# Eight of sixteen weight loads issued from ScalarE's queue instead of SyncE's, in a fused linear attention and soft mixture-of-experts kernel

## The chip, the core and the metric

The kernel runs on one core of one Trainium2 chip. A core has a matrix engine (TensorE, PE in the profile; its weight loads are listed apart as PEld), three engines for element work (VectorE or DVE, ScalarE or ACT, GpSimd or POOL) and SyncE (SP), which in this kernel only issues transfers. Sixteen DMA engines move data between the chip's main memory (HBM) and the core's working memory (SBUF). Each engine runs its own instruction list in order, and the lists wait for one another by semaphores. The metric is the time of one execution on the device in microseconds (us); lower is better.

## What is computed

Linear attention without a softmax, a root-mean-square norm per head, and a soft mixture of experts over all 4608 tokens. The reference, shortened:

```python
def attn(q, k, v, g_norm):                       # 8 batches, 8 heads, 576 tokens, 64 wide
    kv = np.einsum('bhsd,bhse->bhde', k, v)
    out = np.einsum('bhsd,bhde->bhse', q, kv)
    rms = np.sqrt(np.mean(out * out, axis=-1, keepdims=True) + 1e-06)
    return out / rms * g_norm

def moe(x, phi, w1, w2):                         # x: 4608 x 512; 8 experts, 4 slots each, hidden 1024
    logits = x @ phi
    d = softmax over tokens of logits
    slot_input = (d.T @ x).reshape(8, 4, 512)
    for e in range(8):
        slot_out[e] = np.maximum(slot_input[e] @ w1[e], 0.0) @ w2[e]
    c = softmax over slots of logits
    return c @ slot_out
```

All inputs are 32-bit floats, and every one of them is read from HBM once.

## The kernel before

**Stages.** The 4608 tokens are cut into 36 tiles of 128 (`NT`), counted by `T`. First comes the loop over `T`: PE multiplies a tile of q with the block-diagonal kv matrices (`products`, L252 and, for the tile that straddles two batches, L243); ScalarE squares the result and copies it out of PE's accumulators (`square` L262, `evict` L269 and L270); VectorE, ScalarE and GpSimd make the norms, scale the tile and form its logits; groups of six tiles feed the softmax over tokens (`group_sum`, L386). In between, `kv_step` makes the kv matrix of the next batch (L184, L199). After the last tile the slot inputs are known, and the experts begin: `expert_h(e)` multiplies with w1 of expert e (L597) and ScalarE applies the ReLU (`h`, L605); `expert_y(e, hf)` multiplies with one half (`hf`) of w2's columns (L615) and adds into one accumulator per half. At last `output` multiplies each half with the softmax over slots (L647), ScalarE and VectorE copy the product to SBUF (L655, L657), and a transfer of 768 KB stores it (L658); there are six for each half, twelve in all.

**What is loaded, and in which order.** q and kv come as transfers of 1 to 2.25 MB (`load_q` L73, `load_kv` L69). The weights come as sixteen units of 2 MB: `("w1", e)` and `("w2", u)`, with e and u from 0 to 7. Each is one transfer of 128 rows of 16 KB, except `("w2", 2)`, which lies in two places and is two transfers of 128 rows of 8 KB. All are issued by `load_w` (L98) on SyncE, in the order w1 0, w2 0, w1 1, w2 1 (behind tile 18), w1 2, w1 3, w1 4 (behind tile 27), w1 5 (behind tile 31), w1 6, w1 7, w2 2 (after the loop), w2 3 (after `expert_h(0)`), w2 4, w2 5 (after `expert_h(1)` and both halves of expert 0), w2 6, w2 7 (after `expert_h(2)` and both halves of expert 1). The short names below are these. The units w2 2 to w2 7 are packed by column half: 2, 3 and 4 hold the first half for experts 2-3, 4-5 and 6-7, and 5, 6 and 7 hold the second half for the same experts.

**What sets the order.** The program is recorded in the order in which it is written, engine by engine; no scheduler moves anything. A load into SBUF space that was used before waits until that use is over (mostly a wait for PE). There are also eight completion semaphores, DMAHW0 to DMAHW7, dealt out in turn, so a transfer waits for the landing of the one that had its semaphore eight transfers earlier. SyncE carries out all of this in order: a load that waits holds up every later load and store.

**PE's order at the end**, on which the prediction leans: h of experts 0 and 1; y of expert 0, both halves; h 2; y of expert 1, both halves; h 3 to h 7; then y of experts 2 to 7 for the first half (needs w2 2, w2 3, w2 4); then y of expert 2, second half (w2 5), `mix(0)`, y of expert 3; outputs 0 and 1; y of experts 4 and 5, second half (w2 6); outputs 2 and 3; y of experts 6 and 7 (w2 7); output 4; `mix(1)`; outputs 5 to 11. In code:

```python
    for e in range(NE - LATE, NE):
        expert_y(e, 0)
    gather(0)
    expert_y(2, 1)
    mix(0)
    expert_y(3, 1)
    output(0, *chunks[0])
    output(0, *chunks[1])
    expert_y(4, 1)
    expert_y(5, 1)
```

Of the kernel before, what the change touches and what calls it, by code (L numbers as in the profile page):

```python
# [48 lines left out]
def soft_moe_linear_attention(ctx: ExitStack, tc: tile.TileContext, kv_in, q_in, w1_in, w2_in, c_in, out):  # L49


    nc = tc.nc
# [11 lines left out]
    def place(at, n):  # L64
        return arena[:, at * KB : at * KB + n]
# [22 lines left out]
    def homes(kind, u):  # L88
        at = W_AT[kind, u]
        if at is None:  # L90
            return [xflat[:, :UNIT]]
        return [place(a, UNIT // len(at)) for a in at]

    def load_w(kind, u):
        parts = homes(kind, u)
        n = UNIT // len(parts)
        for i, t in enumerate(parts):
            nc.sync.dma_start(t, (w1_in if kind == "w1" else w2_in)[u, :, i * n : i * n + n])  # L98

    def w_block(kind, u, i):  # L100
        parts = homes(kind, u)
# [20 lines left out]
    loads_behind = {  # L122
        9: lambda: (load_kv(5), load_kv(6), load_q(3), load_kv(7)),
        18: lambda: [load_w(k, e) for e in range(2) for k in ("w1", "w2")],
        27: lambda: [load_w("w1", e) for e in range(2, 5)],
        31: lambda: load_w("w1", 5),
    }

# [574 lines left out]
def build_program():  # L703
    import concourse.bacc as bacc

    nc = bacc.Bacc("TRN2", target_bir_lowering=False, num_devices=1, dynamic_dma_scratch_size=SCRATCH)
    shapes = {"kv": (B, P, TOK), "qt": (B // 2, P, TOK), "w1": (NE, P, UNIT), "w2": (NE, P, UNIT), "cs": (P, 129)}
    args = [nc.dram_tensor(f"in_{n}_dram", s, F32, kind="ExternalInput").ap() for n, s in shapes.items()]
    args.append(nc.dram_tensor("out_0_dram", (2, NCH, P, 2, 4 * CT * NS), F32, kind="ExternalOutput").ap())
    with tile.TileContext(nc, schedule_with_timeline_sim=True) as tc, tc.manual_schedule():  # L710
        soft_moe_linear_attention(tc, *args)
    return nc
# [43 lines left out]
```

## Time and profile before

| | us |
|---|---|
| median of 3 runs | 176.11 (175.97 to 177.55) |
| the profiled execution, own time | 175.97 |
| span of the profiled execution, first to last instruction | 174.2 |
| PE busy | 148.2 (85% of the span) |
| VectorE busy | 88.3 (51%) |
| ScalarE busy | 86.8 (50%) |
| GpSimd busy | 55.7 (32%) |
| moved by DMA | 71.68 MB, at a mean of 411 GB/s |

The busy times are shares of the span; a share says nothing by itself of what bounds a stage, since engines work beside each other. The page also has the span cut into 40 equal slices, with the busy tenths of each engine and of the DMA engines, and the chain of waits that ended last. A row of the timeline gives start, duration, engine, line, what is written and read, and in brackets how long the engine sat idle before it and what ended the wait. A row on a transfer gives how many were issued in the stretch asked for, their size, and the time from issue until the last byte was reported landed.

### The profile page before, as it was taken

How to read it: one execution, taken by the hardware profiler on the slowest of the kernel's cores; microseconds unless marked ns; L12 is line 12 of the kernel's file. 1: busy time of each engine (PE TensorE's matmuls, PEld its weight loads, DVE VectorE, ACT ScalarE, POOL GpSimd, SP SyncE). 2: the span in 40 equal slices, each digit the busy share in tenths (PEclk: the TensorE clock that was granted, in tenths of full speed). 3: DMA queues.
4: the chain of work that ended last, by engine and by line, in shares of the span. 5: the costliest groups of instructions: out<-in, count | busy, mean ns of one | idle time of the engine just before them, and what ended most of it. 6: DMA issues, size and time to landing. Idle time of an engine off the chain costs nothing.

```text
span 174.2 us, 4772 instructions
## 1 busy us (share of the span) xinstructions
PE 148.2 (85%) x2024; PEld 108.9 (63%) x2024; DVE 88.3 (51%) x180; ACT 86.8 (50%) x224; POOL 55.7 (32%) x65
## 2 busy tenths in 40 slices
PE   7577799999989899999999769989999959989500
PEld 5456778889779788888996555456556424445200
DVE  1122156566486565466663778733888114457600
ACT  2036286986957957878779553102234003336400
POOL 6000067656546676266773568000000000000000
PEclk9999999999999999999999999999999999999955
DMA  5999999999999999999999999999999999999994
GB/s 188 416 429 426 439 414 432 420 432 440 414 432 423 421 431 420 420 427 436 429 418 419 433 418 433 429 429 406 440 421 419 425 425 426 386 398 406 419 419 199
DMA packets 6645, 71.68 MB, mean 411 GB/s; under 512 B 736, under 2 KB 864, under 8 KB 2400
## 3 DMA queue, kind: packets, MB, share of 16 engines
q1 hardware_dynamic: 6624, 71.37, 97.5%
q8 instruction: 16, 0.26, 0.6%
q14 instruction: 5, 0.04, 0.1%
HBM read 61.93 MB, written 9.44 MB: 410 GB/s over the span
## 4 chain that ended last, share of the span: by engine, by line
PE 46%; DMA 20%; ACT 11%; DVE 11%; issue 3%; POOL 2%; SPq 1%; POOLq 0%; DVEq 0%
PE o L252 17%; DMA arena<-in_w_dram 11%; DMA arena<-in_kv_dram 9%; PE kvp_kv L184 8%; PE po L647 5%; PE pY L615 4%; PE ph L597 3%; DVE logits L329 3%; PE pS L386 2%; DVE ms L275 2%; ACT arena L655 2%; POOL part L324 2%; ACT bd L219 2%; PE o L243 2%; ACT sq L262 2%
## 5 line engine op out<-in xcount | busy, mean ns | idle before, releaser
L252 PE MATMUL o<-bd,arena 128*128 128x192 f32 x256 | 49.4, 336 | 1.4 <-ACT xall L270 0.6
L252 PEld LDWEIGHTS o<-bd,arena 128*128 128x128 f32 x256 | 40.8, 190 | 4.7 <-ACT xall L270 1.6
L302 POOL TENSOR_TENSOR xall<-xall,r 128x512 f32<-128x512 f32 x34 | 34.8, 1044 | 0.0
L324 POOL TENSOR_TENSOR part<-part,r 128x512 f32<-128x512 f32 x17 | 17.8, 1049 | 51.5 <-DVE r L293 51.5
L329 DVE TENSOR_REDUCE logits<-part 128x64 f32<-128x512 f32 (+1 forms) x19 | 19.3, 1015 | 16.1 <-POOL part L324 16.0
L275 DVE TENSOR_REDUCE ms<-sq 128x16 f32<-128x1024 f32 (+1 forms) x19 | 22.0, 1156 | 6.2 <-ACT sq L262 6.2
L262 ACT ACTIVATE sq<-o 128x512 f32<-128x512 f32 x36 | 21.5, 596 | 6.5 <-PE o L252 5.9
L270 ACT COPY xall<-o 128x512 f32<-128x512 f32 x34 | 20.6, 607 | 0.0
L184 PE MATMUL kvp_kv<-arena 128*64 128x64 f32 x480 | 17.3, 225 | 3.6 <-DMA arena<-in_kv_dram 3.6
L655 ACT COPY arena<-po 128x768 f32<-128x768 f32 x12 | 9.3, 800 | 20.2 <-DMA arena<-in_w_dram 10.3
L184 PEld LDWEIGHTS kvp_kv<-arena 128*64 128x64 f32 x480 | 15.2, 138 | 6.5 <-DMA arena<-in_kv_dram 4.5
L615 PE MATMUL pY<-arena,xall 128*32 128x256 f32 x256 | 15.2, 380 | 2.4 <-DMA arena<-in_w_dram 2.4
L657 DVE COPY arena<-po 128x768 f32<-128x768 f32 x12 | 11.3, 956 | 8.0 <-PE po L647 7.2
L647 PE MATMUL po<-logits,z 32*128 32x384 f32 x96 | 13.7, 526 | 1.6 <-ACT arena L655 1.0
L615 PEld LDWEIGHTS pY<-arena,xall 128*32 128x32 f32 x256 | 8.0, 110 | 9.1 <-issue 3.2
L597 PE MATMUL ph<-arena,sTe 128*32 128x256 f32 x224 | 12.7, 379 | 0.3 <-DVE sTe L544 0.3
L269 ACT COPY part<-o 128x256 f32<-128x256 f32 x34 | 12.6, 371 | 0.0
L386 PE MATMUL pS<-xall,d 128*32 128x129 f32 x288 | 10.7, 276 | 2.1 <-ACT d L374 2.1
L283 ACT ACTIVATE r<-ms,eps 128x16 f32<-128x16 f32 x17 | 5.2, 308 | 12.8 <-DVE ms L275 12.6
L647 PEld LDWEIGHTS po<-logits,z 32*128 32x128 f32 x96 | 6.3, 183 | 8.2 <-ACT arena L655 4.1
L291 DVE SCALAR_TENSOR_TENSOR r<-ms,r 128x16 f32<-128x16 f32 x17 | 3.0, 175 | 15.3 <-ACT r L284 15.3
L597 PEld LDWEIGHTS ph<-arena,sTe 128*32 128x32 f32 x224 | 7.2, 110 | 5.2 <-DVE sTe L544 0.6
(88 smaller groups left out, 143.9 us busy)
## 6 DMA issues: line engine op xcount, KB each, us to landing
arena<-in_w_dram SPq DMA_DIRECT2D x14, 2048.0 KB, 20.7
arena<-in_kv_dram SPq DMA_DIRECT2D x6, 2304.0 KB, 30.4
out_dram<-arena SPq DMA_DIRECT2D x12, 768.0 KB, 6.5
arena<-in_kv_dram SPq DMA_DIRECT2D x4, 1152.0 KB, 10.1
arena<-in_qt_dram SPq DMA_DIRECT2D x2, 2304.0 KB, 32.1
arena<-in_qt_dram SPq DMA_DIRECT2D x2, 1280.0 KB, 23.2
arena<-in_qt_dram SPq DMA_DIRECT2D x2, 1024.0 KB, 16.4
xall<-in_w_dram SPq DMA_DIRECT2D x1, 2048.0 KB, 15.4
```

The lines of the kernel that those rows point to most:

```text
L184: nc.tensor.matmul(self.pkv[lo : lo + 64, w, g], lhsT=main[:, w, 1, c, lo : lo + 64], rhs=main[:, w, 0, c, lo : lo + 64], start=c == 0 and ...
L252: nc.tensor.matmul(o[:, r, :192], lhsT=q_main(2 * g + i)[:, r, at : at + P], rhs=bds[i][:, r], start=True, stop=True)
L262: nc.scalar.activation(sqs[s][:, T - starts[s]], o[:, :, 32:160], AF.Square, scale=0.125)
L270: nc.scalar.copy(xts[T % NX][:, :, :128], o[:, :, 32:160])
L275: nc.vector.tensor_reduce(out=mss[s], in_=sqs.pop(s).rearrange("p t j (w d) -> p (t j w) d", w=2), axis=AX.X, op=ALU.add)
L302: nc.gpsimd.tensor_tensor(out=x, in0=x, in1=r[:, i].rearrange("p (j w) -> p j w", w=2).unsqueeze(3).to_broadcast([P, 4, 2, D]), op=ALU.mult,)
L324: engine.tensor_tensor(out=part, in0=part, in1=rs_of[s].unsqueeze(3).to_broadcast([P, STAGES[s], H, NS]), op=ALU.mult)
L329: nc.vector.tensor_reduce(out=L[:, pos(starts[s]) : pos(starts[s]) + STAGES[s]], in_=parts.pop(s).rearrange("p t h n -> p t n h"), axis=AX ...
L386: nc.tensor.matmul(pS[32 * j : 32 * j + 32], lhsT=ds[G][:, i], rhs=x[:, j], start=i == 0, stop=i == GROUPS[G] - 1)
L597: nc.tensor.matmul(ph[32 * j : 32 * j + 32], lhsT=sTe[:, (4 * e + c) * NS : (4 * e + c + 1) * NS], rhs=w_block("w1", e, 4 * c + j), start= ...
L615: nc.tensor.matmul(pY[32 * j : 32 * j + 32, hf, :256], lhsT=hTs[e][:, c], rhs=w_block("w2", u, at + c), start=e == 0 and c < 4, stop=e == ...
L647: nc.tensor.matmul(po[:, u, : CT * NS].rearrange("p (g x) -> p g x", g=2), lhsT=z[lo : lo + 32, f * P : (f + 1) * P], rhs=cT[k][lo : lo + 32],
```

## The change

`load_w` looks up each weight unit in a set, `ACT_LOADS`. The eight units in the set are issued from ScalarE's instruction list (`nc.scalar`), the other eight from SyncE's as before. The two lists have a queue each on the same sixteen DMA engines. Sizes, places, and the calls of `load_w` stay the same.

```diff
+    ACT_LOADS = {("w2", 0), ("w2", 1), ("w1", 3), ("w1", 5), ("w1", 7), ("w2", 3), ("w2", 5), ("w2", 7)}
+
     def load_w(kind, u):
+        queue = nc.scalar if (kind, u) in ACT_LOADS else nc.sync
         parts = homes(kind, u)
         n = UNIT // len(parts)
         for i, t in enumerate(parts):
-            nc.sync.dma_start(t, (w1_in if kind == "w1" else w2_in)[u, :, i * n : i * n + n])
+            queue.dma_start(t, (w1_in if kind == "w1" else w2_in)[u, :, i * n : i * n + n])
```

Three lines are added, so line numbers behind them grow by three (L98 becomes L101). On SyncE, from the last loads of q and kv to the stores, the list changes as follows ("-" before, "+" now; `in_w_dram` are the weights, `arena` and `xall` places in SBUF, x9 means nine in a row):

```order
 L73 DMA arena<-in_qt_dram 128x4608
 L69 DMA arena<-in_kv_dram 128x4608
-L98 DMA arena<-in_w_dram 128x4096 x9
-L98 DMA xall<-in_w_dram 128x4096
-L98 DMA arena<-in_w_dram 128x2048 x2
-L98 DMA arena<-in_w_dram 128x4096 x5
-L658 DMA out_dram<-arena 128x1536 x12
+L101 DMA arena<-in_w_dram 128x4096 x5
+L101 DMA arena<-in_w_dram 128x2048 x2
+L101 DMA arena<-in_w_dram 128x4096 x2
+L661 DMA out_dram<-arena 128x1536 x12
```

SyncE now issues w1 0, w1 1, w1 2, w1 4, w1 6, the two parts of w2 2, w2 4 and w2 6, and then the twelve stores.

On ScalarE, at the first experts, the list before reads (h is the ReLU of an expert, ph its product on PE, `logits` the exponential for the softmax over slots):

```order
L605 ACTIVATE h_1482<-ph_1465,rs 128x256 [waits DVE_49,PE_49,Pool_49]
L605 ACTIVATE h_1503<-ph_1486,rs 128x256 [waits PE_49]
L569 ACTIVATE logits<-logits 128x416 [waits DVE_49]
L605 ACTIVATE h_1552<-ph_1535,rs 128x256 [waits PE_49,Activation_49]
L569 ACTIVATE logits<-logits 128x416 [waits DVE_49]
```

and now:

```order
L608 ACTIVATE h_1482<-ph_1465,rs 128x256 [waits DVE_49,PE_49,Pool_49]
L101 DMA arena<-in_w_dram 128x4096 [waits DMAHW5_49,DMAHW1_49]
L608 ACTIVATE h_1503<-ph_1486,rs 128x256 [waits PE_49]
L101 DMA arena<-in_w_dram 128x4096 [waits DMAHW6_49,DMAHW2_49]
L572 ACTIVATE logits<-logits 128x416 [waits DVE_49]
L608 ACTIVATE h_1552<-ph_1535,rs 128x256 [waits PE_49,Activation_49]
L101 DMA arena<-in_w_dram 128x4096 [waits DMAHW0_49]
L572 ACTIVATE logits<-logits 128x416 [waits DVE_49]
```

The three transfers that came in are w2 3, w2 5 and w2 7, behind the ReLU of experts 0, 1 and 2. In front of each stands a wait for landings: DMAHW5 is that of w1 2, DMAHW6 that of w1 4, DMAHW0 that of w1 5, and DMAHW1 and DMAHW2 are those of w1 0 and w1 1, whose space is written over. The other five stand earlier on ScalarE: w2 0 and w2 1 behind the copies of tile 18, w1 3 behind those of tile 27, w1 5 behind those of tile 31, and w1 7 behind the last square root of the norms, where it waits for PE's last reading of its space. PE, VectorE and GpSimd keep their lists; the waits there name other DMAHW semaphores, since these are dealt out anew.

## The prediction

> **What bounds the kernel now.** I read the page's slices first, then the stretches of the second half, then the chain that ended last, then PE's rows at that place. The slices (40 of 4.36 us) show the DMA engines full from the second slice to the last but one:
>
> ```profile
> span 174.2 us, 4772 instructions
> ...
> DMA  5999999999999999999999999999999999999994
> GB/s 188 416 429 426 439 414 432 420 432 440 414 432 423 421 431 420 420 427 436 429 418 419 433 418 433 429 429 406 440 421 419 425 425 426 386 398 406 419 419 199
> ```
>
> The stretches have, per row, the busy time of five engines, the granted clock, the DMA engines' share, and GB/s:
>
> ```profile
> core 0: us, PE busy (x) PEld busy (x) DVE busy (x) ACT busy (x) POOL busy (x), PEclk, DMA share, GB/s
> ...
> 125.00:146.00 21.00, 18.31 (x310) 10.18 (x300) 10.42 (x24) 4.18 (x9) 0.00 (x0) 1.00 1.00 424
> 146.00:151.00 5.00, 4.75 (x52) 2.15 (x52) 2.00 (x3) 1.98 (x3) 0.00 (x0) 1.00 0.97 402
> 151.00:157.00 6.00, 5.49 (x60) 2.67 (x58) 3.52 (x5) 1.97 (x4) 0.00 (x0) 1.00 0.95 393
> 157.00:172.00 15.00, 6.08 (x44) 2.91 (x42) 5.67 (x7) 4.42 (x6) 0.00 (x0) 0.76 0.99 406
> ```
>
> From 125 to 146 the share is 1.00, and the slices say the same of what lies before: the transfers bound the kernel, and PE waits for them. Afterwards it drops to 0.95 to 0.99: here the stores come out of PE, ScalarE and VectorE only about as fast as they can be written. The chain shows that join (start, duration, what):
>
> ```profile
> 125.29 19.77 DMA arena<-in_w_dram
> ...
> 145.07 0.81 ACT arena L655
> ...
> 146.84 1.86 PE pY L615 x32
> ```
>
> So the end is set twice, by bytes and by the chain of outputs that starts at the late halves of w2. PE's rows name the wait before that chain:
>
> ```profile
> 133.68 5.36 PE L615 MATMUL pY<-arena,xall 128*32 128x256 f32 x96
> 141.48 1.07 PE L615 MATMUL pY<-arena,xall 128*32 128x256 f32 x16 [2.44 <-DMA arena<-in_w_dram]
> ...
> 146.77 1.93 PE L615 MATMUL pY<-arena,xall 128*32 128x256 f32 x32
> ```
>
> 133.68 is y of experts 2 to 7, first half, 5.36/3 = 1.8 us per pair, so the pair that needs w2 4 begins at 137.2. 141.48 is y of expert 2, second half, released by w2 5. 146.77 are experts 4 and 5, which need w2 6.
>
> **When the weights land now.** Issue rows of w1 6, w2 4 and w2 6 (in this order), each followed by the row with its size and the us to landing:
>
> ```profile
> 102.10 0.33 SPq L98 DMA_DIRECT2D arena<-in_w_dram  x1
> arena<-in_w_dram SPq DMA_DIRECT2D x1, 2048.0 KB, 14.7
> ...
> 121.84 0.33 SPq L98 DMA_DIRECT2D arena<-in_w_dram  x1
> arena<-in_w_dram SPq DMA_DIRECT2D x1, 2048.0 KB, 14.6
> ...
> 125.29 0.33 SPq L98 DMA_DIRECT2D arena<-in_w_dram  x1
> arena<-in_w_dram SPq DMA_DIRECT2D x1, 2048.0 KB, 20.9
> ```
>
> w1 6 lands at 116.8, w2 4 at 136.4, w2 6 at 146.2. Between the first and the last lie six units in 29.4 us: 4.9 us a unit, strictly one behind the other. w2 7 is due one unit after w2 6, at 151.1.
>
> **Cost on ScalarE.** Each issue takes 0.33 us on SyncE (rows above) to 0.42 (the row of kv 7 below); ScalarE gets eight, some 3 us. Behind each place it sits idle today (the bracket is the idle time before the row):
>
> ```profile
> 63.27 0.60 ACT L262 ACTIVATE sq<-o 128x512 f32<-128x512 f32 x1 [1.11 <-PE o L252]
> 86.61 0.31 ACT L283 ACTIVATE r<-ms,eps 128x16 f32<-128x16 f32 x1 [1.05 <-DVE ms L275]
> 98.11 0.31 ACT L283 ACTIVATE r<-ms,eps 128x16 f32<-128x16 f32 x1 [2.04 <-DVE ms L275]
> 111.79 0.32 ACT L362 ACTIVATE diag<-ident,rmax 128x32 f32<-128x32 f32 x1 [3.41 <-DVE rmax L358]
> 118.44 0.47 ACT L605 ACTIVATE h<-ph,rs 128x256 f32<-128x256 f32 x1 [4.90 <-PE ph L597]
> 120.12 0.47 ACT L605 ACTIVATE h<-ph,rs 128x256 f32<-128x256 f32 x1 [1.20 <-PE ph L597]
> 122.20 0.55 ACT L569 ACTIVATE logits<-logits 128x416 f32<-128x416 f32 x1 [1.61 <-DVE logits L568]
> 126.58 0.55 ACT L569 ACTIVATE logits<-logits 128x416 f32<-128x416 f32 x1 [2.48 <-DVE logits L568]
> ```
>
> In order: w2 0 and w2 1 (0.84 us) before the first row, w1 3, w1 5, w1 7, then (rows six to eight) w2 3, w2 5, w2 7. Every gap is longer than its issue: cost 0. With the cover gone it would be 3 us at most on the path of PE, which today waits 2.44 us for w2 5 anyway. SyncE's eight fewer issues are worth 0 too, since it waits most of the time; w2 2, w2 4 and w2 6 no longer queue behind w1 7, w2 3 and w2 5, and the stores no longer behind w2 7.
>
> **New waits.** Each of the three late issues holds up ScalarE's next ReLU or `logits` until older weights have landed. Taking turns, bytes move at the same rate, so w1 4, the eighth unit that either queue begins behind kv 7 (with part of a ninth beside it), is in at 71.3 (below) + 9 x 4.9 = 115.4 at the latest, and ScalarE asks at 120.12 + 0.47 = 120.6. These waits cost 0.
>
> **What the second queue delays.** w2 0 and w2 1, issued from ScalarE near 62.2 (63.27 - 1.11), no longer stand behind kv 7, which is needed at the row of L184 below:
>
> ```profile
> 36.00 0.42 SPq L69 DMA_DIRECT2D arena<-in_kv_dram  x1
> arena<-in_kv_dram SPq DMA_DIRECT2D x1, 2304.0 KB, 35.3
> ...
> 84.10 0.39 PE L184 MATMUL kvp_kv<-arena 128*64 128x64 f32 x6
> ```
>
> It lands at 71.3 now. Sharing half and half from 63.6 stretches the rest from 7.7 to 15.4 us, to 79.0: still 5 us ahead. Cost 0.
>
> The end is another matter. The total of bytes is unchanged and neither queue runs dry, so the last weight still lands at 151.1; but of two transfers that share, each lands later than if it had gone first. w1 7 goes out from ScalarE after 108.4 (gap of the fourth row above: 111.79 - 3.41) and is through by 120. w2 3 is issued at 118.9 and, with 1.4 us to its start (half of the 2.75 us that the first load, last fence below, takes beyond its moving), begins at 120.3. From there 30.8 us of moving remain: 14.7 for ScalarE's w2 3, w2 5, w2 7, and 16.1 for SyncE's rest of w1 6 (1.4), w2 2, w2 4, w2 6.
>
> - Equal bytes: SyncE's queue runs at half rate, w1 6 to 123.1, w2 2 to 132.9, w2 4 to 142.7; ScalarE's three end at 149.7, and w2 6 at 151.1.
> - Equal turns, row by row: w2 2 has rows of 8 KB against 16 KB, so its 4.9 us take 14.7, to 137.8. By then ScalarE's queue has moved 11.2 of 14.7; the other 3.5 are shared until 144.8, and w2 4, with 1.4 left, lands at 146.2, w2 6 at 151.1.
>
> PE's pair on w2 4 then ends 1.8 us after it, and y of expert 2 starts at 144.5 or 148.0, late by 3.0 or 6.5. In the first case w2 6 (151.1 against 146.77 + 3.0) makes it 4.3; in the second it is there in time. So the chain of outputs is late by 4.3 to 6.5 us, and what is late next is the stores. Once the weights are in, only this chain feeds the DMA engines.
>
> The Trainium skill ("DMA: Bandwidth & Descriptors", section "Queues, rings and completion order") says that each DMA engine goes round robin between queues packet by packet, a packet being typically 9 to 17 descriptors. By that a turn could be a whole unit's share of an engine (8 rows and a completion), which gives w2 4 at 146.2 as well, the later of the two. No run shown here has two data queues at work.
>
> How much of the delay reaches the end follows from the sixth and the last store, and from the first load, which had nothing ahead of it:
>
> ```profile
> 157.17 0.33 SPq L658 DMA_DIRECT2D out_dram<-arena  x1
> out_dram<-arena SPq DMA_DIRECT2D x1, 768.0 KB, 5.1
> ...
> 164.74 0.64 SPq L658 DMA_DIRECT2D out_dram<-arena  x1
> out_dram<-arena SPq DMA_DIRECT2D x1, 768.0 KB, 8.5
> ...
> 0.74 0.37 SPq L69 DMA_DIRECT2D arena<-in_kv_dram  x1
> arena<-in_kv_dram SPq DMA_DIRECT2D x1, 1152.0 KB, 5.5
> ```
>
> The sixth lands at 162.3, the last at 173.2: six in 10.9 us, 1.8 each, so from the sixth on the writing sets the pace. The sixth itself took 5.1 us; into an idle queue it would take 1.8 plus something between 0 and the first load's 5.5 - 2.75 = 2.75 us. The slack before a late chain shows at the end is thus 0.5 to 3.3 us; with no row nearer to either end I take the middle, 1.9. Sum: 4.3 - 1.9 = +2.4 us, or 6.5 - 1.9 = +4.6; the middle is +3.5. The execution profiled took 175.97 us, 0.14 below the median: 175.97 + 3.5 = 179.5. Its own range is +1.0 (equal bytes, all slack) to +6.0 (row turns, least slack): 177.0 to 182.0.
>
> **Rivals.**
> - The second queue changes nothing: the units come through one after another, w2 4 by 139.7 (141.48 - 1.8) and w2 6 by 148.7 (146.77 and the slack), and bytes bind as before. Time 176.0, within 0.5. For it: a share of 1.00 before 146, which no queue can improve or harm while it is fed. Against: w2 4 would have to pass two units issued before it. The Trainium skill's section "Issuing engines are not separate DMA queues" of the same page speaks for this and against any gain: all issuing engines use the same sixteen DMA engines, and a second one saves only issue time. The share of 1.00 agrees.
> - Turns cost time. The one foreign traffic in the trace is instruction fetches:
>
> ```profile
> q1 hardware_dynamic: 6624, 71.37, 97.5%
> q8 instruction: 16, 0.26, 0.6%
> ```
>
>   0.6% of 16 engines' 174.2 us over 16 packets of 16 KB is 1.05 us each, against 4.9/8 = 0.61 for a weight row: 0.44 more. Of a unit's 128 rows each engine moves 8, so ScalarE's eight units are 64 rows on each; if every one paid that, 28 us: 204. An eighth of it on top of the forecast is 183. Against: instructions go elsewhere than data.
> - ScalarE is held up. If w1 4 came after 120.6, the ReLU of expert 2 and all behind it would be late with it. It decides only from 9 us on (137.2 to 146.2, where PE waits anyway): each further us adds one, 180 and more.
> - Faster: two queues move more. The best slice has 440 GB/s, the stretch up to 146 424. Over the 87.5 us from 63.6 to 151.1 that would take 3.0 us off: 173. It decides (over 1%) from 434 GB/s, and only if w2 4 and w2 6 come no later than now. Against it, the share leaves no idle time to win.
>
> **How the numbers follow.** About 1% is what a measurement here can tell from no change. Forecast 0.52, of which 0.07 lies below that bound; nothing changes 0.25; turns cost 0.13; ScalarE held up 0.04; faster 0.06. Slower by over 1%: 0.45 + 0.13 + 0.04 = 0.62; within 1%: 0.32; faster: 0.06. The range 175.4 to 183.5 holds the forecast and nearly all of the second case, and leaves out the faster case and most of the dear turns.
>
> **What would show it.** Right: in the changed profile PE waits before the pair on w2 4 (L618), y of expert 2 starts at 144 to 148, DMA share below 0.95 between 147 and 157, w2 0 lands before kv 7, and no DMA wait on ScalarE's rows before the outputs. Wrong: y of expert 2 near 141.5 (rival one), GB/s under 400 between 64 and 146 (turns cost), L608 waiting for a DMA (ScalarE held up), GB/s over 434 (faster).

## The result and the profile after

The changed kernel takes 182.55 us (median of 4 runs, 180.88 to 184.51), the kernel before 176.04 (175.91 to 177.55): a ratio of 1.032, 95% interval 1.021 to 1.042, so slower. The forecast was 179.5 with a range of 175.4 to 183.5. Here and below, a ratio compares the means of those executions that lie within 1.5% of the fastest of their kernel (here without 184.51), so it need not be the ratio of the medians. The profiled execution after took 183.07 us with a span of 181.0; of before it was 175.97 and 174.2.

The page's slices of the kernel after (40 of 4.53 us) show where the time lies:

```profile
span 181.0 us, 4774 instructions
...
PEclk9999999999999999999999999999999579999975
DMA  6999999999999999999999999999999970889993
GB/s 200 414 428 422 443 416 438 411 442 407 444 428 423 421 422 427 425 429 416 438 424 418 431 424 434 420 411 425 434 422 424 431 319 36 348 349 403 414 414 162
```

Up to the 32nd slice nothing differs from before: engines full, 407 to 444 GB/s. Then there is a hole (36 GB/s) that was not there, and just ahead of it the granted clock of TensorE dips to a half. The stretches, with the columns of before (busy time of the five engines, granted clock, DMA share, GB/s):

```profile
64.00:100.00 36.00, 35.16 (x502) 29.63 (x494) 22.00 (x46) 27.26 (x77) 19.62 (x21) 1.00 1.00 425
...
125.00:146.00 21.00, 14.22 (x254) 9.66 (x250) 9.00 (x21) 3.36 (x7) 0.00 (x0) 0.87 1.01 428
146.00:151.00 5.00, 4.46 (x58) 1.88 (x50) 0.85 (x2) 0.00 (x0) 0.00 (x0) 0.87 0.51 216
151.00:157.00 6.00, 5.75 (x64) 2.63 (x60) 2.36 (x3) 2.01 (x3) 0.00 (x0) 1.00 0.54 221
```

Between 146 and 157 the share is 0.51 and 0.54, where it was 0.97 and 0.95. Only the engines that are behind still load (w2 6 lands at 151.2, w2 7 at 151.3), and there is nothing to store until 153.06, because PE is late. PE's rows at that place say what it waited for:

```profile
134.20 3.66 PE L618 MATMUL pY<-arena,xall 128*32 128x256 f32 x62
144.65 3.19 PE L618 MATMUL pY<-arena,xall 128*32 128x256 f32 x32 [6.78 <-DMA arena<-in_w_dram]
148.38 1.07 PE L618 MATMUL pY<-arena,xall 128*32 128x256 f32 x16 [0.54 <-DVE y L634]
149.38 0.70 PE L638 MATMUL pz<-y,sel 128*128 128x256 f32 x2
```

The first row is two pairs; the second is the pair on w2 4, which was due straight behind them and now waits 6.78 us. Behind it y of expert 2, second half, starts at 148.38, against 141.48. The chain that ended last agrees (start, duration, what; these rows are the longer pieces of that stretch):

```profile
122.37 22.14 DMA arena<-in_w_dram
144.65 3.23 PE pY L618 x32
148.38 1.07 PE pY L618 x16
153.74 1.86 PE pY L618 x32
```

The issues of the late units, each with the row of its time to landing, for w2 3 and w2 5 (ScalarE) and w2 4 (SyncE, whose issue row groups w2 4 and w2 6):

```profile
118.83 0.34 ACTq L101 DMA_DIRECT2D arena<-in_w_dram  x1
arena<-in_w_dram ACTq DMA_DIRECT2D x1, 2048.0 KB, 13.0
...
120.48 0.33 ACTq L101 DMA_DIRECT2D arena<-in_w_dram  x1
arena<-in_w_dram ACTq DMA_DIRECT2D x1, 2048.0 KB, 21.6
...
122.37 3.78 SPq L101 DMA_DIRECT2D arena<-in_w_dram  x2
arena<-in_w_dram SPq DMA_DIRECT2D x1, 2048.0 KB, 22.1
```

w2 3 lands at 131.8 and w2 5 at 142.1, within 0.8 us of before, but w2 4 at 144.5 instead of 136.4: it now lands behind w2 5, which PE needs only in the step after it. How the two queues shared can be read from their packets, bytes and share of engine time between 123 and 129, where SyncE's queue (q1) moves the rest of w2 2 in rows of 8 KB, and ScalarE's (q10) moves w2 3 in rows of 16 KB:

```profile
q10 hardware_dynamic: 105, 1.72, 67.8%
q1 hardware_dynamic: 96, 0.84, 33.5%
```

About as many packets each, but twice the bytes for the queue with the longer rows. The 96 are 59 rows of 8 KB, 15 packets of 4 bytes that report an engine's share of a transfer as done, and 22 rows of 16 KB, since the engines that are ahead have already begun w2 4. The packets of the trace show the turns themselves: sorted by start and end they form sixteen chains without gaps, one for each engine, and between 124 and 142 us 522 of 540 neighbours in a chain come from different queues. One row of one queue is followed by one row of the other.

### The profile page after: what moved, and what is told of

Same layout as the page of the kernel before. It is cut to its first block, busy times and chain, and to the rows that moved or that the text cites. A ratio compares the mean times of both kernels' runs of the same rounds, so it can differ in the third digit from the quotient of the medians.

```text
span 181.0 us, 4774 instructions
## 1 busy us (share of the span) xinstructions
PE 149.7 (83%) x2024; PEld 111.2 (61%) x2024; DVE 88.2 (49%) x180; ACT 86.9 (48%) x224; POOL 55.6 (31%) x65
## 4 chain that ended last, share of the span: by engine, by line
PE 50%; DMA 21%; ACT 11%; DVE 8%; issue 3%; POOL 2%; SPq 1%; POOLq 0%; DVEq 0%
PE o L255 16%; DMA arena<-in_w_dram 12%; DMA arena<-in_kv_dram 8%; PE kvp_kv L187 8%; PE pY L618 6%; PE po L650 6%; PE pS L389 3%; PE fill L432 3%; PE ph L600 2%; ACT arena L658 2%; DVE logits L332 2%; POOL part L327 2%; ACT bd L222 2%; PE o L246 2%; ACT sq L265 2%
## 5 line engine op out<-in xcount | busy, mean ns | idle before, releaser
L618 PE MATMUL pY<-arena,xall 128*32 128x256 f32 x256 | 17.4, 405 | 7.3 <-DMA arena<-in_w_dram 6.8
L618 PEld LDWEIGHTS pY<-arena,xall 128*32 128x32 f32 x256 | 9.3, 116 | 14.5 <-issue 9.9
L600 PEld LDWEIGHTS ph<-arena,sTe 128*32 128x32 f32 x224 | 8.4, 110 | 4.1 <-DVE sTe L547 0.6
```

The lines of the kernel that those rows point to most:

```text
L600: nc.tensor.matmul(ph[32 * j : 32 * j + 32], lhsT=sTe[:, (4 * e + c) * NS : (4 * e + c + 1) * NS], rhs=w_block("w1", e, 4 * c + j), start= ...
L618: nc.tensor.matmul(pY[32 * j : 32 * j + 32, hf, :256], lhsT=hTs[e][:, c], rhs=w_block("w2", u, at + c), start=e == 0 and c < 4, stop=e == ...
```

## The experiments

Times are medians, each with the ratio to the kernel before in the same session. That kernel's own median was 177.35, 176.03 and 176.02 us in the three sessions; the last two experiments bear on why it moves.

**The early five alone.** w2 3, w2 5 and w2 7 go back to SyncE.

```diff
-    ACT_LOADS = {("w2", 0), ("w2", 1), ("w1", 3), ("w1", 5), ("w1", 7), ("w2", 3), ("w2", 5), ("w2", 7)}
+    ACT_LOADS = {("w2", 0), ("w2", 1), ("w1", 3), ("w1", 5), ("w1", 7)}
```

> Five units stay on ScalarE's queue (w2 0, w2 1, w1 3, w1 5, w1 7), the last three (w2 3, w2 5, w2 7) go back to SyncE. Theory: the loss comes only from w2 2 and w2 4 sharing with units that are needed later; here the last units come one behind the other again, so w2 4 lands by 137, y of expert 2 (second half) starts near 141.5, and the span is 174 to 175. Rival (each unit on the second queue costs by itself): five eighths of the 6.8 us of span remain, 178.4.

Measured: 176.37 us, ratio 0.999 (0.995 to 1.002). The five early transfers on the second queue cost nothing and win nothing. Its profiled execution took 216.64 us at a granted clock of 0.65 and can't be compared row by row; the same kernel, profiled once more:

> The same kernel as that with five units on ScalarE's queue, for a profile at full clock: w2 2 to w2 7 land about 4.9 us apart, w2 4 by 137, w2 6 by 147, y of expert 2 (second half) near 141.5, span 174 to 175. Rival: 178.4.

Its span is 175.7 us and its time 177.81. w2 4, w2 5 and w2 6 land at 136.4, 141.3 and 146.2, as before. Its PE rows show that 1.5 us were lost at another place:

```profile
141.45 1.20 PE L618 MATMUL pY<-arena,xall 128*32 128x256 f32 x16 [2.38 <-DMA arena<-in_w_dram]
142.58 1.22 PE L638 MATMUL pz<-y,sel 128*128 128x256 f32 x2
143.73 1.94 PE L618 MATMUL pY<-arena,xall 128*32 128x256 f32 x16
```

The weights come as in the kernel before, but the matmuls behind the wait are slower: 1.94 us for 16 against 1.07. This is taken up in the last two experiments.

**The late three alone.** The reverse set.

```diff
-    ACT_LOADS = {("w2", 0), ("w2", 1), ("w1", 3), ("w1", 5), ("w1", 7), ("w2", 3), ("w2", 5), ("w2", 7)}
+    ACT_LOADS = {("w2", 3), ("w2", 5), ("w2", 7)}
```

> Only the last three units (w2 3, w2 5, w2 7) go out from ScalarE. Theory: the turns at the end are as in the changed kernel, w2 2 near 134, w2 4 between 144 and 146, y of expert 2 (second half) near 148, span 180 to 182. Rival (each unit costs by itself): three eighths of 6.8 us, 176.8.

Measured: 183.01 us, ratio 1.033 (1.026 to 1.039): the whole loss, with a span of 181.1 as expected. The wait on w2 4 is there again:

```profile
144.36 3.43 PE L618 MATMUL pY<-arena,xall 128*32 128x256 f32 x32 [6.91 <-DMA arena<-in_w_dram]
148.34 1.07 PE L618 MATMUL pY<-arena,xall 128*32 128x256 f32 x16 [0.54 <-DVE y L634]
```

**Short rows on ScalarE's queue.** If the queues take turns row by row, ScalarE's late units in rows of 8 KB should leave SyncE's queue half of the bytes, and w2 4 should come earlier. If they share bytes, nothing should move. Each of the three is split into two homes, and so into two transfers.

```diff
-    ("w2", 3): (72,), ("w2", 5): (104,), ("w2", 7): (136,),
+    ("w2", 3): (72, 80), ("w2", 5): (104, 112), ("w2", 7): (136, 144),
```

> The changed kernel, but w2 3, w2 5 and w2 7 are each two transfers with rows of 8 KB. Theory of turns by row: SyncE's queue then has an equal share while w2 2 moves and two thirds while w2 4 moves; w2 2 lands near 133, w2 4 near 140, w2 5 near 143.4, y of expert 2 (second half) starts near 143.5, span near 176.2. Rival (turns by bytes): nothing changes, w2 4 near 144.5, span 181.

Measured: 179.33 us, ratio 1.014 (1.008 to 1.020), span 178.2. w2 2 lands at 130.3 instead of 134.7, w2 4 at 137.7 instead of 144.5. Turns by rows hold. The span expected (176.2) was missed by two us. w2 5 came in two parts, the second at 146.4 only, and the groups behind the wait were slow (1.43 and 1.77 us for 1.07):

```profile
144.00 1.43 PE L618 MATMUL pY<-arena,xall 128*32 128x256 f32 x16 [2.44 <-DMA arena<-in_w_dram]
145.36 1.22 PE L638 MATMUL pz<-y,sel 128*128 128x256 f32 x2
146.51 1.77 PE L618 MATMUL pY<-arena,xall 128*32 128x256 f32 x16
```

y of expert 3 reads that second part. With the balance moved, the next unit in the line is the late one.

**One queue, another order.** This is the test of the mechanism without a second queue: SyncE issues everything, but w2 5 and w2 7 ahead of w2 4 and w2 6.

```diff
     halves(0)
-    load_w("w2", 4)
     load_w("w2", 5)
     combine(0)
     expert_h(2)
     halves(1)
-    load_w("w2", 6)
     load_w("w2", 7)
+    load_w("w2", 4)
+    load_w("w2", 6)
```

> One queue, all loads on SyncE, but w2 5 and w2 7 are issued ahead of w2 4 and w2 6. Theory (the order in which the units land is the whole cost): w2 4 lands near 146.2, y of expert 2 (second half) starts near 149.5 with a slow pair ahead of it, span 181 to 182. Rival (a second queue costs in itself, beside the order): w2 4 as late, but the span stays under 178.

Measured: 185.44 us, ratio 1.053 (1.047 to 1.058), span 183.5. The units land one behind another every 4.9 us, w2 4 at 146.2, and PE does what it did with two queues:

```profile
133.63 3.64 PE L615 MATMUL pY<-arena,xall 128*32 128x256 f32 x64
146.34 3.64 PE L615 MATMUL pY<-arena,xall 128*32 128x256 f32 x32 [9.07 <-DMA arena<-in_w_dram]
```

So an order of landing alone makes such a loss, here a larger one with w2 4 still 1.7 us later; a second queue is one way to change the order. The span is 1.5 us or more over what was expected. The second row has part of the reason: 3.64 us for a pair that takes 1.8 in the row above (3.64 for two). For the rest, the first store and the last landing are both 9.0 us later than in the kernel before: nothing was swallowed at the end.

**The clock behind the wait.** After the wait, the pair took 3.19 us in the changed kernel too. The stretches around it, first of the kernel after, then of the one-queue order just shown (the third column from the end is the granted clock):

```profile
139.00:141.50 2.50, 0.00 (x0) 0.00 (x0) 0.00 (x0) 0.00 (x0) 0.00 (x0) 0.79 1.02 426
141.50:144.00 2.50, 0.00 (x0) 0.00 (x0) 0.00 (x0) 0.00 (x0) 0.00 (x0) 0.50 1.00 426
144.00:146.00 2.00, 1.35 (x16) 0.78 (x20) 0.00 (x0) 0.00 (x0) 0.00 (x0) 0.50 1.04 442
146.00:148.50 2.50, 1.96 (x28) 0.87 (x24) 0.42 (x1) 0.00 (x0) 0.00 (x0) 0.75 0.79 334
```

```profile
146.00:148.50 2.50, 2.16 (x24) 1.18 (x28) 0.00 (x0) 0.00 (x0) 0.00 (x0) 0.50 0.78 334
```

The clock falls to 0.50 while PE idles and is still there when the pair starts. To test whether that makes the pair slow, 30 matmuls on zeros fill the wait of the changed kernel; they belong to no result.

```diff
     for e in range(NE - LATE, NE):
+        if e == 6:
+            fill(30, home=ps.tile([P, 2, 512], F32, tag="m", name="warm")[:, 0], cols=512)
         expert_y(e, 0)
```

> The changed kernel, with 30 matmuls on zeros (0.224 us each, 6.7 us) put into PE's wait for w2 4; they feed nothing. Theory: the pair of matmul groups behind the wait took 3.19 us and not 1.8 because the granted clock had dropped in the idle time; kept busy, it takes 1.8, and the span is 1.4 us shorter, 179.6. Rival (the slow pair has another cause, or the stores hide it): span 181.

Measured: 180.72 us, ratio 1.021 (1.015 to 1.028), span 178.5. That is 1.8 us under the changed kernel's median, though its four executions (180.48 to 181.01) reach the changed kernel's lowest (180.88); the rows are the firmer evidence:

```profile
137.16 6.65 PE L432 MATMUL warm<-zeros 128*128 128x512 bf16 x30
144.09 1.93 PE L618 MATMUL pY<-arena,xall 128*32 128x256 f32 x32 [0.28 <-DMA arena<-in_w_dram]
146.56 1.07 PE L618 MATMUL pY<-arena,xall 128*32 128x256 f32 x16 [0.54 <-DVE y L634]
```

The granted clock stays at 1.00, and the pair takes 1.93 us again. Of the 2.5 us that the profiled span is shorter, 1.3 are the pair (3.19 - 1.93) and 0.56 that w2 4 happened to land earlier (144.65 - 144.09); the other 0.7 are one DMA engine that lags less at the last store, below.

**How much delay the stores swallow.** The prediction subtracted 1.9 us for that. Zeros (9 for 2 us, 18 for 4 us) are put into the kernel before, ahead of the first output.

```diff
     mix(0)
     expert_y(3, 1)
+    fill(9, home=ps.tile([P, 2, 512], F32, tag="m", name="late")[:, 0], cols=512)
     output(0, *chunks[0])
```

> The kernel before, with 9 matmuls on zeros (0.224 us each, 2.0 us) on PE ahead of output 0; they feed nothing. The chain of outputs is late by 2.0 us. Slack of 1.9 us, as in the prediction: the span grows by 0.1. No slack, as the changed kernel's trace suggests (chain 6.9 late, end 6.8 late): by 2.0.

Measured: 177.51 us, ratio 1.009 (1.003 to 1.014), six executions at 177.1 to 177.6 and four at 179.3 to 179.9. In the profile (177.45) the first store is issued 2.0 us later (148.15), and the span is 1.5 longer. The run with twice the zeros:

> The same with 18 matmuls, 4.0 us. Slack of 1.9 us: the span grows by 2.1. No slack: by 4.0.

Measured: 179.15 us, ratio 1.018 (1.011 to 1.024). In the profile (180.42, the longest of the four) the first store is 5.45 us later (its y of expert 3 met a dropped clock too), and the last lands 4.45 later. So 0.5 us are swallowed of 2.0 and 1.0 of 5.45; why not equally much is taken up with the prediction. The first store's issue, in this order of before, 9 zeros, 18 zeros:

```profile
146.15 19.23 SPq L658 DMA_DIRECT2D out_dram<-arena  x12
```

```profile
148.15 19.26 SPq L658 DMA_DIRECT2D out_dram<-arena  x12
```

```profile
151.60 19.29 SPq L658 DMA_DIRECT2D out_dram<-arena  x12
```

**The zeros in the kernel before.** The kernel before has a wait of its own in front of y of expert 2 (2.44 us). Here nine zeros fill it.

```diff
+    fill(9, home=ps.tile([P, 2, 512], F32, tag="m", name="warm")[:, 0], cols=512)
     gather(0)
     expert_y(2, 1)
```

> The kernel before (one queue) with nine matmuls on zeros (0.22 us each, 2.0 us) in the wait of 2.44 us ahead of y of expert 2, second half, so that PE does not idle there. Theory (what differs between executions of the kernel before is whether the pairs behind this wait run at a dropped clock): the pair of expert 3 takes 1.6 to 1.8 us in every execution, first store issued at 145.9 to 146.3, and all times lie near the lower of the kernel before's, 175.8 to 176.3. Rival (the difference comes from the writing of the last stores): times spread as before, some at 177.5. Third: the zeros end too late and push the chain: first store after 146.5, 176.5 or more.

Measured: 176.01 us, ratio 0.998 (0.994 to 1.001), no difference in the median. The spread differs: ten executions lie between 175.96 and 176.18. Of the kernel before, in the same session, twelve lie between 175.87 and 176.06, six between 177.38 and 177.62, and one at 179.08. No execution near 177.5 of that kernel was profiled, so a dropped clock is the likely reason for this spread, but it was not seen in rows. The PE rows with the zeros:

```profile
139.07 2.12 PE L429 MATMUL warm<-zeros 128*128 128x512 bf16 x9
141.67 1.07 PE L615 MATMUL pY<-arena,xall 128*32 128x256 f32 x16 [0.49 <-DMA arena<-in_w_dram]
...
143.30 1.07 PE L615 MATMUL pY<-arena,xall 128*32 128x256 f32 x16
```

The same zeros with the early five on ScalarE's queue:

> Five early transfers on ScalarE's queue (w2 0, w2 1, w1 3, w1 5, w1 7), the late three on SyncE's, and the same nine matmuls on zeros ahead of y of expert 2, second half. Theory: as the one-queue kernel with the zeros, 175.8 to 176.5, since bytes bind and the late order is the one of before; ratio 0.99 to 1.002. Rival (the five early issues are worth something, or cost something, that the clock hid): 175 or less, or 177 or more.

Measured: 176.22 us, ratio 0.999 (0.996 to 1.002), ten executions between 175.97 and 176.79. So nothing that was tried is faster than the kernel before; with the early five or the zeros the time can't be told from its own, and the zeros only take away the executions at 177.5.

## Why the prediction was right, and where its sum was off

**The mechanism was right.** Bytes bind until 146, the total is the same, and the loss lies in the order: w2 4 waits for its turns while ScalarE's queue moves units that are needed later. The late three alone carry all of it (183.01 against 182.55), and one queue with the order changed loses as well (185.44).

**Equal turns, not equal bytes.** The prediction put w2 4 at 142.7 by the one and at 146.2 by the other. It landed at 144.5, and the 105 against 96 packets with 1.72 against 0.84 MB, as well as the short rows (w2 4 at 137.7), decide for rows. It came 1.7 us ahead of 146.2 because w2 2 was through at 134.7, not at 137.8: the prediction let the sharing begin at 120.3, but ScalarE's first row of w2 3 starts at 122.3, and by 122.6 the engines have moved 175 of the 256 rows of w2 2. That w2 6 would be late next could then not matter: it landed at 151.2, and was needed at 153.7.

The Trainium skill ("DMA: Bandwidth & Descriptors", section "Queues, rings and completion order") lets an engine drain a packet of typically 9 to 17 descriptors before it turns to the next queue. The prediction made of it a turn of a whole share, eight rows and a report. The chains above show neither: 522 of 540 neighbours change the queue after a single row (or report). So a turn is one row here, whatever its bytes, and SyncE's queue with rows of 8 KB got the smaller half.

**Costs that were put at nothing.** ScalarE: its rows show `h` at 120.42 with the same idle of 1.20 us ahead of it as before, and no wait for a DMA. Its rows come some 0.3 us later than before, but they do so at 55 us already, ahead of its first issue. An issue stands beside the ReLU, inside its time:

```profile
118.75 0.47 ACT L608 ACTIVATE h<-ph,rs 128x256 f32<-128x256 f32 x1 [4.90 <-PE ph L600]
118.83 0.34 ACTq L101 DMA_DIRECT2D arena<-in_w_dram  x1
120.42 0.47 ACT L608 ACTIVATE h<-ph,rs 128x256 f32<-128x256 f32 x1 [1.20 <-PE ph L600]
```

kv 7 landed at 77.5 instead of 71.3, later as worked out (79.0), and still ahead of its use at 84.4. Turns cost no rate: 425, 424 and 428 GB/s before 146.

**What was mis-sized.** y of expert 2 was put at 144.5 to 148.0 and started at 148.38, late by 6.9 us. Three parts make that up. w2 4 came late by 5.0: 144.65 + 1.8 for a pair at full clock is 146.45, against 141.48. The pair at the dropped clock added 1.4 (3.19 - 1.8), and PE now waits 0.5 for the copy of y (L634), which the wait for w2 5 hid before. The prediction had the first part (4.3 to 6.5) and neither of the others. It priced the pair at 1.8 us, from rows in which PE had no wait ahead of it. One row it misread: the chain of before has a DMA end at 145.06, ahead of the first output copy, but no unit lands then (w2 5 at 141.3, w2 6 at 146.2). The chain after has PE's first output product in that place (151.08 to 151.95, copy at 151.97), which fits PE's row at 144.11 before. The sum did not use that row.

The slack of the stores, 1.9 us in the middle of 0.5 to 3.3, was the step that failed most. All of the 6.9 came through: the last store lands at 180.06 instead of 173.23, 6.83 later. With the zeros the slack was 0.5 and 1.0. What is left of it can be seen in the bytes of the last stores, from 171.6 us on in slices of 0.235 us, first before, then after:

```profile
GB/s 209 209 209 131 52 0 0 0 0 0 0 0 0 35 0 0 0 0 0 0 0 0 0 0 0 0 0 0 0 0 0 0 0 0 0 0 0 0 0 0
```

```profile
GB/s 418 418 392 418 419 418 418 418 444 418 418 418 419 418 418 418 418 418 418 418 419 418 418 418 418 418 418 392 53 26 26 26 26 26 0 0 0 0 0 0
```

Before, half of the engines had landed by 172.0 and the others by 173.2; after, all but one had landed by 178.8, and one (26 of 418 GB/s) at 180.06. The engines that are ahead have no backlog: their share of the sixth store lands 3.1 us after its issue in both kernels (157.17 to 160.28, 164.08 to 167.21). So the 5.1 us of the sixth store, from which the prediction read a backlog, was that of the engines that lag, by 1.6 us at the last store. After, fifteen had caught up, but one lagged 1.3 all the same.

Taken apart like this, the runs agree. The fifteen were later than the last landing before (173.23) by 0.6, 4.1 and 5.5 us (9 zeros, 18 zeros, kernel after), where the first store was later by 2.0, 5.45 and 6.9: 1.4 us were swallowed each time. In the one-queue order it is 1.4 too (7.7 of 9.0). What differs is the sixteenth engine, which landed another 0.9, 0.4, 1.3 and 1.4 us behind the fifteen. In the kernel after it falls behind at the fifth store (fifteen land by 165.36, one at 167.28). Five packets follow each other there without a gap: store rows of 0.45, 0.46 and 0.37 us, an instruction fetch of 0.96 (at 164.77) and a store row of 0.60. A store row takes 0.24 otherwise, so these cost 1.9 us more, which is the lag. The other three traces have a fetch where their lag opens as well. The trace does not name the engine of a packet, so that the fetch makes the lag is a close fit, not shown by a run without it.

So the prediction's 1.9 us was some 0.5 too much for the fifteen engines, and left out that one late engine can undo nearly all of it.

With the least slack (0.5) and equal turns, the prediction's sum was +6.0, its upper end, and 6.5 was measured between the medians: 182.55 lies outside the sum's own range, which ended at 182.0. The stated range held the time because it reached on to 183.5 for the turns that cost time, and these did not come. That is luck. The three sizes that were off (the clock, the copy of y, the slack) all made the loss larger.

## What to carry to other kernels

When bytes bind, a second queue moves none of them faster; it changes the order in which transfers land, and the one that is needed first now shares with those needed later. Leave the last units on one queue in the order of their use; or, as the turns suggest but no run here tried, give the queue of the urgent transfer the longer rows. When a forecast adds a wait ahead of matmuls, price them at half the clock as well, and take a backlog of stores from the engine that is ahead, not from the one that lands last.

## What the runs showed of the chip

- The granted clock fell to 0.50 at 140.4, 2.6 us after PE's last matmul (137.9), and was back at 1.00 at 147.2, 2.6 us after the pair had begun. In the one-queue order it fell 3.0 us after the last matmul and came back after 4.2 us at work. After that wait of 9.07 us the pair took 3.64 us, exactly twice 1.82. The Trainium skill ("TensorE: Matmul & The Clock Gate", part "The HAM clock gate") puts the half clock behind at least one idle window of some 3.4 us. A shorter wait can do it too: in the second profile of the early five, PE idled 2.38 us, and the clock was at 0.50 from 142.3 to 145.7, with 1.94 instead of 1.07 us for a group. In the profile of the kernel before, a wait of 2.44 us left it at 1.00. So the length of a wait does not decide alone. These three spells at half clock lasted 6.83, 10.24 and 3.41 us, whole multiples of the shortest.
- ScalarE's issue rows start inside the time of its activations (118.83 beside the ReLU of 118.75): what they cost it does not show in its rows.
- With two queues the sixteen engines drift apart. Their shares of w2 4 landed between 135.6 and 144.5 in the kernel after, and between 132.7 and 136.5 before. Of the 81 rows of w2 2 left when the sharing began (at 122.6), the engines that were ahead had few and those behind had many, each now followed by a row of the other queue: the shares of its second part landed from 123.6 to 134.7. A unit is there only with its last engine, so sharing delays it by more than the mean.
- Two queues with work took turns row by row on each engine: 522 of 540 neighbours between 124 and 142 us, rows of 8 KB and of 16 KB alike.
